# Windowed attention in front of a GELU layer: query halves of 64 with 192 keys each, instead of 128 queries with 256 keys

## The chip, the cores and the metric

The kernel runs on one core of one Trainium2 chip. The metric is the device time of one execution in microseconds (us), as the median of several runs. Five engines work side by side, each through its own instructions in order: TensorE (PE; its weight loads are listed apart as PEld), VectorE (DVE), ScalarE (ACT), GpSimd (POOL) and SyncE (SP), which here only issues loads. They wait for each other by semaphores. A matmul multiplies weights held in the array with columns that stream through it; its result goes to PSUM, which has eight banks.

## The reference

```python
# q, k, v: [4, 8, 768, 64]; n_global = 8, n_local = 96
scores = scale * np.matmul(q, k.transpose(0, 1, 3, 2))
rel = pos[:, None] - pos[None, :]
is_global = pos[None, :] < int(n_global)
is_local = (rel >= 0) & (rel < int(n_local))
keep = is_global | is_local
dist = np.where(is_global & ~is_local, float(n_local), np.abs(rel))
scores = scores + (-slopes[:, None, None] * dist[None])       # slopes: one per head
scores = np.where(keep, scores, -1000000000.0)
a = softmax(scores)                                           # over the keys
attn_out = np.matmul(a, v)
x = attn_out.transpose(0, 2, 1, 3).reshape(4 * 768, 512)
h = x @ w_in                                                  # 512 -> 2048
g = 0.5 * h * (1.0 + erf(h * inv_sqrt2))
return (g @ w_out).astype(np.float32)                         # 2048 -> 512
```

A query sees at most the 96 keys that end at its own place, and the first 8 keys of its sequence.

## The kernel before

The 3072 rows are cut into 12 chunks of 256 rows (`c`); three chunks make one sequence of the batch, so chunks 0, 3, 6 and 9 are a sequence's first ("first chunks") and the others are "later chunks". A chunk has four pairs of heads (`p`); the two heads of a pair (`hh`) lie in partitions 0 to 63 and 64 to 127 of the transposed queries and keys. Within a chunk `j` is the half of 128 queries.

Per pair, attention goes through these steps. `load` (L241) issues the loads of q, k and v on SP, six for a pair of a later chunk and three for one of a first chunk. `split` (L274) scales the queries on POOL. `scores_pair` (L281) multiplies: for each `j` and head, 128 queries by 256 keys (in a later chunk 32 keys from the start of the sequence and the 224 keys from 96 before the half to its end; in a first chunk the first half has 128 keys and the second 256). The product is fp32, with 64 rows and 128 weight columns, so the two heads of a pair use the upper and the lower half of the array's rows. VectorE adds the mask `pen` and finds the row minimum (L305). `exps` (L315) takes the exponentials on ScalarE, sums them, and scales by the inverse sums on POOL (on VectorE for chunks 0 and 1). `flip` (L339) transposes the probabilities in blocks of 128 by 128 on PE, four a head (three in a first chunk), and ScalarE copies them out of PSUM. `av_pair` (L353) multiplies the values, 128 keys by 64 columns as weights, with these blocks, so that the two heads use the left and the right half of the array's columns. ScalarE evicts the sum (`xh`, L382) and VectorE takes the rest (`xl`, L158).

The GELU layer runs in steps `T`, each of one slice `s` of 256 of the 2048 inner columns and one chunk: `m1` (L385, `h`, 24 matmuls), `gelu` (L400, twice on ScalarE) and `m2` (L411, `acc`, 12 matmuls of 512 columns). Chunks 0 and 1 take turns by slice while the weights come in; from chunk 2 on a chunk's eight slices follow each other. The weights arrive as 64-bit words in 32 pieces of 512 KB (`load_weights`, four a slice), which ScalarE and VectorE take apart (L188 to L212).

Which step of attention stands beside which GELU step is set by tables of offsets:

```python
EVS = {"load": (-4, -3, 0, 1), "split": (-2, -1, 2, 3), "s": (0, 0, 4, 4), "pt": (2, 3, 6, 7), "av": (4, 4, 8, 8)}
EVENTS = [EVF, EVF, EV2] + [EVS] * (NCH - 3)
```

From chunk 3 on (`EVS`), every fourth step has a block: av of two pairs, then s of two pairs, in one run on PE. Chunk 2 (`EV2`) goes pair by pair, and chunks 0 and 1 (`EVF`) stand ahead of the GELU steps. Tiles in PSUM come from a pool of six banks (`ps`), taken in turn; `acc` has two of its own. In `run` SP's order begins with chunk 0, the four pieces of weight slice 0, the four pairs of chunk 1, and then the slices 1 to 6. A scheduler sets the final order on each engine.

## Time and profile before

| what | value |
|---|---|
| runs | 719.08, 717.80, 718.84 us; median 718.84 |
| profiled execution, first to last instruction (span) | 719.0 us |
| PE busy | 695.4 us (97%), 4909 matmul records |
| PEld busy | 612.0 us (85%) |
| ACT busy | 371.4 us (52%) |
| DVE busy | 291.4 us (41%) |
| POOL busy | 114.9 us (16%) |
| DMA | 68.03 MB, mean 95 GB/s |
| TensorE's granted clock | 0.987 of full speed as a mean |

The span is that of one profiled execution, and the runs beside it lie within 1.3 us of it, so sums made from the profile can be set against the runs directly. Busy time of PE counts overlapping matmuls once, and a matmul's end is modelled; how fast PE really goes is read from the starts of the blocks, not from busy time.

### The profile page before, as it was taken

The numbers are of one execution on the slowest core, as the hardware profiler recorded it, in microseconds if no ns is written. First come the engines' busy times: TensorE is split into PE (matmuls) and PEld (weight loads), VectorE is DVE, ScalarE is ACT, GpSimd is POOL, SyncE is SP. The second block draws the span as 40 slices with busy tenths as digits, with TensorE's granted clock in tenths as the row PEclk, the third lists the DMA queues.
The fourth block names the chain that finished last, engine by engine and source line by source line (L and its number), as shares of the span: only waits on it lengthen the run. The fifth ranks groups of instructions, "written<-read, shape, count | busy, mean of one in ns | idle before, by whom it ended". The sixth has DMA issues, their size and how long they took to land.

```text
span 719.0 us, 12918 instructions
## 1 busy us (share of the span) xinstructions
PE 695.4 (97%) x4909; PEld 612.0 (85%) x4909; DVE 291.4 (41%) x957; ACT 371.4 (52%) x838; POOL 114.9 (16%) x227
## 2 busy tenths in 40 slices
PE   7888989999999999999999999999999999999996
PEld 4567878788898898899898898988988988998895
DVE  6988988612423324323323324133243243231110
ACT  4885678826535626536436446356356365453211
POOL 3001123302202202012022022022022020120000
PEclk9998999999999999999999999999999999999999
DMA  8527863304324313204224223223233221000000
GB/s 284 156 88 233 264 185 139 111 8 132 103 66 126 104 58 119 74 30 130 80 71 134 90 72 101 84 67 89 88 103 103 88 74 31 30 2 1 31 0 34
DMA packets 60901, 68.03 MB, mean 95 GB/s; under 512 B 13472, under 2 KB 49312, under 8 KB 60832
## 3 DMA queue, kind: packets, MB, share of 16 engines
q1 hardware_dynamic: 56560, 59.92, 28.3%
q10 hardware_dynamic: 4272, 7.21, 2.7%
q8 instruction: 41, 0.67, 0.4%
q14 instruction: 28, 0.23, 0.1%
HBM read 60.82 MB, written 6.29 MB: 93 GB/s over the span
## 4 chain that ended last, share of the span: by engine, by line
PE 84%; ACT 6%; DVE 3%; DMA 3%; POOL 1%; issue 1%; ACTq 0%; DVEq 0%; SPq 0%; POOLq 0%
PE h L396 35%; PE acc L426 34%; PE av L370 5%; PE s L295 5%; PE t L346 5%; ACT n L322 3%; DMA w<-w 2%; POOL n L331 1%; ACT L322 1%; ACT w L188 1%; DVE wb L198 1%; DVE wb L196 1%; DVE n L331 1%; DMA nn_w<-limits 0%; DVE wb L194 0%
## 5 line engine op out<-in xcount | busy, mean ns | idle before, releaser
L396 PE MATMUL h<-xh,winh 128*128 128x256 f32 x768 | 221.9, 289 | 0.8 <-ACT xh L382 0.8
L396 PE MATMUL h<-xl,winh 128*128 128x256 f32 x768 | 218.3, 284 | 0.0
L396 PE MATMUL h<-xh,winl 128*128 128x256 f32 x768 | 217.5, 283 | 0.0
L158 DVE TENSOR_TENSOR gl<-gr,gh 128x512 fp32r<-128x512 f32 x96 | 67.9, 707 | 344.0 <-ACT gr L407 344.0
L426 PE MATMUL acc<-wouth,gh 128*128 128x512 f32 x384 | 156.2, 407 | 4.8 <-ACT gh L406 4.8
L396 PEld LDWEIGHTS h<-xh,winh 128*128 128x128 f32 x768 | 147.6, 192 | 6.6 <-issue 1.8
L396 PEld LDWEIGHTS h<-xl,winh 128*128 128x128 f32 x768 | 147.7, 192 | 4.2 <-DVE n L331 0.3
L426 PE MATMUL acc<-woutl,gh 128*128 128x512 f32 x384 | 151.2, 394 | 0.0
L426 PE MATMUL acc<-wouth,gl 128*128 128x512 f32 x384 | 149.8, 394 | 0.1
L396 PEld LDWEIGHTS h<-xh,winl 128*128 128x128 f32 x768 | 147.4, 192 | 0.1
L406 ACT ACTIVATE gh<-h 128x512 fp32r<-128x512 f32 x96 | 57.3, 597 | 164.7 <-PE h L396 164.6
L350 ACT COPY pt<-t 128x512 f32<-128x512 f32 (+1 forms) x96 | 52.8, 553 | 110.3 <-PE t L346 110.2
L152 POOL TENSOR_SCALAR qr<-qr,qsc 128x256 f32<-128x256 f32 x48 | 28.1, 586 | 459.5 <-DMA qr<-qT 390.1
L331 POOL TENSOR_SCALAR n<-n,su 128x256 f32<-128x256 f32 (+1 forms) x160 | 83.9, 543 | 65.6 <-DVE su L325 26.7
L426 PEld LDWEIGHTS acc<-wouth,gh 128*128 128x128 f32 x384 | 72.3, 188 | 23.7 <-issue 5.8
L426 PEld LDWEIGHTS acc<-wouth,gl 128*128 128x128 f32 x384 | 72.1, 188 | 16.9 <-DVE gl L158 0.8
L426 PEld LDWEIGHTS acc<-woutl,gh 128*128 128x128 f32 x384 | 72.4, 189 | 12.8 <-issue 0.3
L322 ACT ACTIVATE n<-n,mn 128x256 f32<-128x256 f32 (+1 forms) x144 | 68.7, 479 | 0.7 <-DVE mn L305 0.5
L305 DVE CUSTOM_DVE_ANT_0 n<-s,pen 128x256 f32<-128x256 f32 (+1 forms) x192 | 65.8, 397 | 7.7 <-PE s L295 6.0
L346 PE MATMUL t<-ident,n 128*128 128x128 f32 x352 | 57.6, 282 | 5.2 <-DVE n L331 4.3
L407 ACT ACTIVATE gr<-h 128x512 f32<-128x512 f32 x96 | 56.8, 592 | 0.0
L370 PE MATMUL av<-pt,vr 128*64 128x128 f32 x704 | 51.9, 283 | 4.6 <-ACT pt L350 4.5
(68 smaller groups left out, 561.2 us busy)
## 6 DMA issues: line engine op xcount, KB each, us to landing
w<-w SPq DMA_DIRECT2D x32, 512.0 KB, 4.7
c<-w SPq DMA_DIRECT2D x32, 512.0 KB, 3.7
kr<-kT SPq DMA_DIRECT2D x32, 224.0 KB, 3.1
out<-o ACTq DMA_DIRECT2D x24, 256.0 KB, 2.0
qr<-qT SPq DMA_DIRECT2D x45, 128.0 KB, 2.8
vr<-v SPq DMA_DIRECT2D x44, 128.0 KB, 2.3
vr<-v SPq DMA_DIRECT2D x32, 96.0 KB, 2.3
kr<-kT SPq DMA_DIRECT2D x13, 128.0 KB, 2.6
```

Source lines behind the costliest of these rows:

```text
L158: return self.nc.vector.tensor_tensor(out=out, in0=in_, in1=hi.bitcast(F32), op=ALU.subtract)
L295: ins = nc.tensor.matmul(sp[hh][:, j, :w], lhsT=qq[hr, j * P:(j + 1) * P], rhs=kt[hr, 0 if first else j, :w], start=True, stop=True).ins
L305: ins = nc.vector.tensor_tensor_reduce(out=nn[:, j, :w], in0=sp[hh][:, j, :w], in1=pen, scale=-slope(2 * p + hh), scalar=3e38, op0=ALU.add ...
L322: self.table(nc.scalar.activation(out=nn[:, j, :w], in_=nn[:, j, :w], func=AF.Exp, bias=mn[:, i:i + 1], scale=-1.0, accum_out=su[:, i:i + 1]))
L331: ins = eng.tensor_scalar(out=nn[:, j, :w], in0=nn[:, j, :w], scalar1=su[:, i:i + 1], scalar2=0.0, op0=ALU.mult, op1=ALU.add)
L346: nc.tensor.transpose(tp[:, i, :], nn[:, j, a * P:(a + 1) * P], self.ident)
L350: nc.scalar.copy(pt, tp[:, :n, :])
L370: ins = nc.tensor.matmul(av[64 * hh:64 * hh + 64, j, :], lhsT=vt[hh][:, vi, :], rhs=pt[hh][:, i, :], start=(j, a) == js[0], stop=(j, a) == ...
L396: nc.tensor.matmul(hp[:, f, :], lhsT=w[:, d, f * P:(f + 1) * P], rhs=x[:, d, :], start=n == 0, stop=n == 3 * NP - 1)
L406: self.table(nc.scalar.activation(out=gh, in_=hp, func=AF.Gelu))
L407: self.table(nc.scalar.activation(out=gr, in_=hp, func=AF.Gelu))
L426: nc.tensor.matmul(acc, lhsT=g[:, f, ks], rhs=w[:, f, :], start=s == 0 and n == 0, stop=s == NST - 1 and n == 5)
```

## The change

The 128 queries of a half become two quarters of 64 (`a`). A quarter's keys are 64 + 32 + 96 = 192 (`NK`): 32 from the start of the sequence, the 96 that both quarters share around their border, and 64 of its own. The loads put the keys of a half side by side so that each quarter's 192 can be read as two runs of 96 (`pairs`). A score matmul then has 64 weight columns and 192 streamed columns, and the four matmuls of a half (two heads, two quarters) name four different quarters of the array. In a first chunk the first half of 128 queries keeps its form.

The probabilities of a half are then 192 wide, and the two halves of a head take three transposes of 128 by 128: the shared 128 keys of each half, and one block with the 64 own keys of both halves. The values are loaded in four blocks to match (two shared, two of own keys). `av_pair` multiplies the shared keys as before, and then the own keys with 64 rows, 64 weight columns and 64 streamed columns, on quarters of the array; the halves `j` go to PSUM banks of their own in later chunks, and are evicted apart. From chunk 3 on it does both pairs of a block at the second of them. A pair of a later chunk has twelve loads instead of six; the mask is one tile of 448 columns.

```diff
+def pairs(t, off, step, n):
+    return bass.AP(tensor=t.tensor, offset=t.offset + off, ap=[list(t.ap[0]), [step, 2], [1, n]])
...
+    def load_v(self, dma, vv, v0, cc, w):
+        row = lambda r, n: dap(self.v, v0 + r * DM, [[DM, n], [1, w]])
+        q0 = cc * CT
+        if cc:
+            dma(vv[0:NC, 0, :], row(q0 - 32, NC))
+            dma(vv[NC:P, 0, :], row(0, NG))
+        else:
+            dma(vv[:, 0, :], row(0, P))
+        dma(vv[0:NG, 1, :], row(0, NG))
+        dma(vv[NG:P, 1, :], row(q0 + 96, NC))
+        for j in range(2) if cc else (1,):
+            o = HQ * j if cc else 0
+            dma(vv[o:o + HQ, 2:4, :],
+                dap(self.v, v0 + (q0 + j * P - 96) * DM, [[DM, HQ], [160 * DM, 2], [1, w]]))
...
-            sync(kr[:, :, NG:256], dap(self.kT, k0 + cc * CT - 96, [[S, P], [P, 2], [1, 224]]))
-            sync(kr[:, :, 0:NG], dap(self.kT, k0, [[S, P], [0, 2], [1, NG]]))
...
+            sync(pairs(kr, NG, 352, NX + NC), dap(self.kT, q0 - 96, [[S, P], [192, 2], [1, NX + NC]]))
+            sync(kr[:, 224:288], dap(self.kT, q0 + HQ, [[S, P], [1, NX]]))
+            sync(kr[:, KW:KW + NX], dap(self.kT, q0 + 32, [[S, P], [1, NX]]))
+            for o in (0, 192):
+                sync(pairs(kr, o, 352, NG), dap(self.kT, k0, [[S, P], [0, 2], [1, NG]]))
+        self.load_v(sync, vr.rearrange("p n h d -> p n (h d)"), v0, cc, P)
...
         for j in range(2):
-            w = P if first and j == 0 else 256
-            for hh in range(2):
-                hr = slice(hh * D, hh * D + D)
-                ins = nc.tensor.matmul(sp[hh][:, j, :w], lhsT=qq[hr, j * P:(j + 1) * P],
-                                       rhs=kt[hr, 0 if first else j, :w], start=True, stop=True).ins
...
+            for a in range(1 if first and j == 0 else 2):
+                for hh in range(2):
+                    hr = slice(hh * D, hh * D + D)
+                    if first and j == 0:
+                        out, lhs, rhs = sp[hh][:, 0, 0:P], qq[hr, 0:P], kt[hr, 0:P]
+                    else:
+                        o = j * P + a * HQ
+                        out, lhs = sp[hh][a * HQ:(a + 1) * HQ, j, :], qq[hr, o:o + HQ]
...
-        tp = self.bank([P, 4, P], f"t{c}_{h}")
-        for i, (j, a) in enumerate(pts):
-            nc.tensor.transpose(tp[:, i, :], nn[:, j, a * P:(a + 1) * P], self.ident)
+        tp = self.bank([P, 3, P], f"t{c}_{h}")
+        for i, o in enumerate((0, 2 * P, NK if c % CPB == 0 else P)):
+            nc.tensor.transpose(tp[:, i, :], nn[:, o:o + P], self.ident)
...
+        if first:
+            avb = self.bank([P, 2, n, P], f"av{c}_{p}")
+            av = [avb[:, j] for j in range(2)]
+        else:
+            av = [self.bank([P, n, P], f"av{c}_{p}_{j}") for j in range(2)]
...
+        for i in range(n):
+            for j in range(2):
+                for hh in range(2):
+                    pt, vt = heads[i, hh]
+                    add(av[j][hh * D:(hh + 1) * D, i, :], vt[:, j, :], pt[:, j, :],
+                        i == 0 and (j == 0 or not first), first and j == 0)
+        for i in range(n):
+            for a in range(2):
+                for j in range(2):
+                    if first and j == 0:
+                        continue
+                    ks = slice(0, HQ) if first else slice(j * HQ, (j + 1) * HQ)
+                    for hh in range(2):
+                        pt, vt = heads[i, hh]
+                        qs = slice(a * HQ, (a + 1) * HQ)
+                        add(av[j][hh * D:(hh + 1) * D, i, qs], vt[ks, 2 + a, :], pt[ks, 2, qs], False, True)
+        for j in range(2):
+            xh, xl = (x[:, ps.start:ps.stop, j * P:(j + 1) * P] for x in self.x[c])
+            nc.scalar.copy(xh, av[j])
+            self.lo_dve(xl, av[j], xh)
```

Lines shift: what is L295 (s), L346 (t), L370 (av), L396 (h) and L426 (acc) before stands at L337, L382, L412, L449 and L479 in the changed kernel.

On PE, this is the block in chunk 4 in which av of the pairs 0 and 1 and s of the pairs 2 and 3 follow each other, as it stood before. A name such as `s4_6` is the tile of chunk 4, head 6; the size is that of the output.

```order
L370 MATMUL av4_0_2698<-pt4_0_2552,vr4_0_2062 64x128 x8
L370 MATMUL av4_0_2698<-pt4_2_2611,vr4_1_2181 64x128 x8
L295 MATMUL s4_4_2719<-kr4_2_2353,qr4_2_2354 128x256
L295 MATMUL s4_5_2720<-kr4_2_2353,qr4_2_2354 128x256
L295 MATMUL s4_4_2719<-kr4_2_2353,qr4_2_2354 128x256
L295 MATMUL s4_5_2720<-kr4_2_2353,qr4_2_2354 128x256
L295 MATMUL s4_6_2733<-kr4_3_2470,qr4_3_2471 128x256
L295 MATMUL s4_7_2734<-kr4_3_2470,qr4_3_2471 128x256
L295 MATMUL s4_6_2733<-kr4_3_2470,qr4_3_2471 128x256
L295 MATMUL s4_7_2734<-kr4_3_2470,qr4_3_2471 128x256
L426 MATMUL acc3_0_2578<-wouth2_712,gh29_2625 128x512
```

The same block on PE in the changed kernel, up to the first scores of pair 2:

```order
L412 MATMUL av4_1_0_2925<-pt4_0_2776,vr4_0_2239 64x128 x2
L412 MATMUL av4_1_1_2926<-pt4_0_2776,vr4_0_2239 64x128 x2
L412 MATMUL av4_1_0_2925<-pt4_2_2833,vr4_1_2374 64x128 x2
L412 MATMUL av4_1_1_2926<-pt4_2_2833,vr4_1_2374 64x128 x2
L412 MATMUL av4_1_0_2925<-pt4_0_2776,vr4_0_2239 64x64 x2
L412 MATMUL av4_1_1_2926<-pt4_0_2776,vr4_0_2239 64x64 x2
L412 MATMUL av4_1_0_2925<-pt4_0_2776,vr4_0_2239 64x64 x2
L412 MATMUL av4_1_1_2926<-pt4_0_2776,vr4_0_2239 64x64 x2
...
L337 MATMUL s4_4_2957<-kr4_2_2552,qr4_2_2553 64x192
L337 MATMUL s4_5_2958<-kr4_2_2552,qr4_2_2553 64x192
L337 MATMUL s4_4_2957<-kr4_2_2552,qr4_2_2553 64x192
L337 MATMUL s4_5_2958<-kr4_2_2552,qr4_2_2553 64x192
```

The 16 matmuls of av of 128 columns became 8 of 128 columns and 16 of 64; the 8 of s became 16 of half the height and 192 columns. The order of the parts is the same.

On PE, in a first chunk (chunk 3), the scores of pair 2 in the changed kernel stand between av and the scores of pair 3:

```order
L412 MATMUL av3_1_2285<-pt3_2_2193,vr3_1_1774 64x64 x4
L337 MATMUL s3_4_2308<-kr3_2_1943,qr3_2_1944 128x128
L337 MATMUL s3_5_2309<-kr3_2_1943,qr3_2_1944 128x128
L337 MATMUL s3_4_2308<-kr3_2_1943,qr3_2_1944 64x192
L337 MATMUL s3_5_2309<-kr3_2_1943,qr3_2_1944 64x192
L337 MATMUL s3_4_2308<-kr3_2_1943,qr3_2_1944 64x192
L337 MATMUL s3_5_2309<-kr3_2_1943,qr3_2_1944 64x192
L337 MATMUL s3_6_2324<-kr3_3_2057,qr3_3_2058 128x128
```

Here matmuls of the old form (128 rows of output) and of the new one follow each other in turn.

On SP, the loads of the last pair of chunk 1 and the first pieces of weight slice 1 stood like this before:

```order
L246 DMA qr_3_199<-qT 128x256
L246 DMA kr_3_198<-kT 128x2x224
L246 DMA kr_3_198<-kT 128x2x32
L246 DMA vr_3_200<-v 128x2x128
L246 DMA vr_3_200<-v 96x2x128
L246 DMA vr_3_200<-v 32x2x128
L163 DMA w_0_207<-w 128x1024
L163 DMA w_1_209<-w 128x1024
```

and stand like this in the changed kernel:

```order
L279 DMA qr_3_226<-qT 128x256
L279 DMA kr_3_225<-kT 128x2x160
L279 DMA kr_3_225<-kT 128x64 x2
L279 DMA kr_3_225<-kT 128x2x32 x2
L279 DMA vr_3_227<-v 96x128
L279 DMA vr_3_227<-v 32x128 x2
L279 DMA vr_3_227<-v 96x128
L279 DMA vr_3_227<-v 64x2x128 x2
L178 DMA w_0_240<-w 128x1024
L178 DMA w_1_242<-w 128x1024
```

Twelve loads stand where six stood, for each of the four pairs, and the weights of slice 1 come behind all of them as before.

## Rows read from the trace of the kernel before

**Rows 1.** The head of the page, and its chain of work that ended last: shares of the span by engine and by line.
```profile
span 719.0 us, 12918 instructions
...
PE 84%; ACT 6%; DVE 3%; DMA 3%; POOL 1%; issue 1%; ACTq 0%; DVEq 0%; SPq 0%; POOLq 0%
PE h L396 35%; PE acc L426 34%; PE av L370 5%; PE s L295 5%; PE t L346 5%; ACT n L322 3%; DMA w<-w 2%; POOL n L331 1%; ACT L322 1%; ACT w L188 1%; DVE wb L198 1%; DVE wb L196 1%; DVE n L331 1%; DMA nn_w<-limits 0%; DVE wb L194 0%
```

**Rows 2.** Busy time by stretch of the span: start and end, length, then PE, PEld, DVE, ACT and POOL busy with the number of instructions, the granted clock of TensorE, the DMA engines' share and GB/s.
```profile
0.00:30.00 30.00, 22.66 (x124) 14.74 (x125) 22.12 (x93) 17.13 (x56) 7.96 (x27) 0.89 0.79 246
30.00:60.00 30.00, 25.63 (x194) 19.79 (x194) 26.94 (x83) 24.05 (x58) 0.00 (x0) 0.94 0.35 107
60.00:95.00 35.00, 30.22 (x180) 26.55 (x179) 29.51 (x59) 24.20 (x44) 8.13 (x7) 0.95 0.81 247
95.00:130.00 35.00, 34.11 (x224) 28.49 (x224) 28.86 (x64) 27.01 (x55) 11.86 (x13) 0.95 0.48 154
130.00:700.00 570.00, 569.94 (x4123) 511.51 (x4122) 182.60 (x661) 275.62 (x623) 87.00 (x181) 1.00 0.26 75
```

**Rows 3.** Who PE waited for over the whole span, longest first: us in total, times, longest us.
```profile
PE acc L426 <- ACT gh L406: 4.8, 2, 2.4
PE av L370 <- ACT pt L350: 4.5, 4, 2.0
PE t L346 <- DVE n L331: 4.3, 3, 2.3
```

**Rows 4.** The chain in order of time around a block of a later chunk: start us, us, what, and how many records.
```profile
291.53 0.44 PE t L346 x4
291.96 2.75 PE acc L426 x12
...
297.58 1.90 PE av L370 x32
299.48 1.93 PE s L295 x16
301.41 2.95 PE acc L426 x12
```

**Rows 5.** The same around a block of a first chunk.
```profile
347.30 0.33 PE t L346 x3
...
353.27 1.46 PE av L370 x24
354.73 1.51 PE s L295 x16
```

**Rows 6.** Groups of ScalarE's instructions with different shapes kept apart, over the whole span: line, operation, output<-input, shapes, count | busy us, mean ns of one | idle us before and what ended it.
```profile
L406 ACT ACTIVATE gh<-h 128x512 fp32r<-128x512 f32 x96 | 57.3, 597 | 164.7 <-PE h L396 164.6
L407 ACT ACTIVATE gr<-h 128x512 f32<-128x512 f32 x96 | 56.8, 592 | 0.0
...
L382 ACT CAST xh<-av 128x256 fp32r<-128x256 f32 x12 | 4.3, 360 | 12.2 <-PE av L370 12.1
```

**Rows 7.** SP's issues in order of time while chunk 1 is loaded: start us, us, and how many of one line and tile follow each other. The rows between are the pairs' loads of k and v.
```profile
5.12 0.43 SPq L246 DMA_DIRECT2D qr<-qT  x1
...
12.43 0.35 SPq L246 DMA_DIRECT2D qr<-qT  x1
...
16.20 0.42 SPq L246 DMA_DIRECT2D qr<-qT  x1
...
19.18 0.42 SPq L246 DMA_DIRECT2D qr<-qT  x1
...
22.21 1.30 SPq L163 DMA_DIRECT2D w<-w  x2
```

**Rows 8.** From the rows of the weight pieces `w` between 20 and 45 us: the time from issue to landing.
```profile
DMA to landing us min/median/max: 3.5/3.6/4.7
```

**Rows 9.** ScalarE takes the first piece of weight slice 1: its row in order of time on ScalarE (a wait would stand in brackets), and its row in the chain.
```profile
33.19 0.66 ACT L188 ACTIVATE w<-w 128x512 int32<-128x512 uint32 x1
...
33.28 0.56 ACT w L188
```

**Rows 10.** Groups of ScalarE's and VectorE's instructions between 0 and 60 us with shapes kept apart, columns as in rows 6.
```profile
L322 ACT ACTIVATE n<-n,nmax 128x256 f32<-128x256 f32 x24 | 11.9, 498 | 0.7 <-DVE nmax L305 0.6
L350 ACT COPY pt<-t 128x512 f32<-128x512 f32 x8 | 4.4, 575 | 2.0 <-PE t L346 2.0
L350 ACT COPY pt<-t 128x384 f32<-128x384 f32 x8 | 3.6, 467 | 0.8 <-PE t L346 0.8
L322 ACT ACTIVATE n<-n,nmax 128x128 f32<-128x128 f32 x8 | 3.1, 394 | 9.2 <-DVE nmax L305 9.2
...
L305 DVE CUSTOM_DVE_ANT_0 n<-s,pen 128x256 f32<-128x256 f32 x24 | 9.3, 418 | 0.6 <-POOL pen L135 0.6
L331 DVE TENSOR_SCALAR n<-n,su 128x256 f32<-128x256 f32 x24 | 7.3, 348 | 0.1
L331 DVE TENSOR_SCALAR n<-n,su 128x128 f32<-128x128 f32 x8 | 2.4, 302 | 0.1
L305 DVE CUSTOM_DVE_ANT_0 n<-s,pen 128x128 f32<-128x128 f32 x8 | 2.3, 284 | 0.4 <-PE s L295 0.4
```

**Rows 11.** The chain in order of time between 100 and 130 us, one step on POOL: start us, us, what.
```profile
109.15 3.55 POOL n L331 x3
```

**Rows 12.** Busy time in the middle of an av block of a later chunk, columns as in rows 2.
```profile
326.00:327.40 1.40, 1.40 (x30) 1.40 (x28) 0.44 (x1) 0.93 (x2) 0.00 (x0) 1.00 0.00 0
```

More of the change, by code (lines that the diff above doesn't have):

```diff
@@ L23 @@
 NG = 32
+HQ = 64
+NX = 64
+NC = 96
+NK = NX + NG + NC
+KW = NC + 2 * (NX + NG)
 CT = 256
@@ L288, in scores_pair @@
         kt, qq = self.kt.pop((c, p)), self.qt.pop((c, p))
[L289 removed]
+        sp = [self.bank([P, 2, NK], f"s{c}_{2 * p + hh}") for hh in range(2)]
         prev = self.last_av if EVENTS[c] is not EVF else None
         for j in range(2):
[L292 to L299 removed]
+            for a in range(1 if first and j == 0 else 2):
[7 more added lines that the diff above has]
+                        if first:
+                            rhs = pairs(kt[hr, :], 192 if a else 288, -96 if a else -192, NC)
+                        elif j == 0:
+                            rhs = pairs(kt[hr, :], 96, 96 if a else -96, NC)
+                        else:
+                            rhs = pairs(kt[hr, :], KW + 192 * a, -96 if a else 96, NC)
+                    ins = nc.tensor.matmul(out, lhsT=lhs, rhs=rhs, start=True, stop=True).ins
+                    if prev is not None:
+                        self.after(ins, prev, "heads and halves in turn")
+                    prev = ins
@@ L318, in exps @@
         mn, su = self.stat.pop((c, p))
-        every = [(self.pt_n[c, 2 * p + hh], j, P if first and j == 0 else 256, 2 * hh + j)
+        every = [(self.pt_n[c, 2 * p + hh][:, j * NK:j * NK + (P if first and j == 0 else NK)], 2 * hh + j)
                  for hh in range(2) for j in range(2)]
-        for nn, j, w, i in every:
-            self.table(nc.scalar.activation(out=nn[:, j, :w], in_=nn[:, j, :w], func=AF.Exp, bias=mn[:, i:i + 1],
+        for nn, i in every:
+            self.table(nc.scalar.activation(out=nn, in_=nn, func=AF.Exp, bias=mn[:, i:i + 1],
                                             scale=-1.0, accum_out=su[:, i:i + 1]))
@@ L359, in av_pair @@
                          self.xp.tile([P, NP, CT], F32R, name=f"xl{c}", tag="xl"))
-        pts = self.parts(c)
-        pt = [self.pt_t.pop((c, 2 * p + hh)) for hh in range(2)]
-        vt = [self.vt.pop((c, 2 * p + hh)) for hh in range(2)]
-        if p % 2 == 0 or EVENTS[c] is not EVS:
-            self.avb = self.bank([P, 2, 2, P], f"av{c}_{p}")
-        av = self.avb[:, p % 2]
-        for i, (j, a) in enumerate(pts):
-            vi = (a if first else 2 * j + a)
-            js = [x for x in pts if x[0] == j]
-            for hh in range(2):
-                ins = nc.tensor.matmul(av[64 * hh:64 * hh + 64, j, :], lhsT=vt[hh][:, vi, :], rhs=pt[hh][:, i, :],
-                                       start=(j, a) == js[0], stop=(j, a) == js[-1]).ins
-                if self.last_av is not None and i + hh > 0:
-                    self.after(ins, self.last_av, "two heads in turn")
-                self.last_av = ins
-        ps = slice(p, p + 1)
         if EVENTS[c] is EVS:
@@ L378, in av_pair, with add @@
                 return
-            ps = slice(p - 1, p + 1)
-        xh, xl = (x[:, ps, :].rearrange("d p (j q) -> d p j q", j=2) for x in self.x[c])
-        av = self.avb[:, ps.start % 2:ps.start % 2 + ps.stop - ps.start]
-        nc.scalar.copy(xh, av)
-        self.lo_dve(xl, av, xh)
+            ps = range(p - 1, p + 1)
+        else:
+            ps = range(p, p + 1)
+        n = len(ps)
+        if first:
+            avb = self.bank([P, 2, n, P], f"av{c}_{p}")
+            av = [avb[:, j] for j in range(2)]
+        else:
+            av = [self.bank([P, n, P], f"av{c}_{p}_{j}") for j in range(2)]
+        heads = {(i, hh): (self.pt_t.pop((c, 2 * q + hh)), self.vt.pop((c, 2 * q + hh)))
+                 for i, q in enumerate(ps) for hh in range(2)}
+        def add(out, lhs, rhs, start, stop):
+            ins = nc.tensor.matmul(out, lhsT=lhs, rhs=rhs, start=start, stop=stop, skip_group_check=True).ins
+            if self.last_av is not None:
+                self.after(ins, self.last_av, "heads and halves in turn")
+            self.last_av = ins
+        for i in range(n):
[18 more added lines that the diff above has]
+            self.lo_dve(xl, av[j], xh)
     def m1(self, t, f):
```

87 lines of the change are left out of this document (41 added, 46 removed).

## The prediction

> **What bounds the kernel now.** I read the page's chain first: 84% of it is TensorE, and of the lines that the change touches the chain holds av, s and t with 5% each [rows 1]. The table by stretch says where that is so: from 130 us to 700 us PE is busy for 569.94 of 570 us at granted clock 1.00, while ScalarE and VectorE are half busy or less; before 130 us PE is idle for some 17 us, with VectorE and DMA the fuller ones at different times [rows 2]. So there are two regimes. Behind 130 us a microsecond off PE's attention blocks is a microsecond off the end; ahead of it, it is worth that only where PE is what the others wait for. PE is idle there for softmax results, for copies and for Gelu inputs [rows 3].
>
> In the first regime the chain gives the price of every block directly, without modelled ends. A block of two pairs in a chunk that is not a batch's first ("later chunk") costs av 1.90 us and s 1.93 us, and each head's four transposes cost 0.44 us; the products with w_out just behind s take 2.95 us instead of 2.75 us [rows 4]. In a batch's first chunk the same block is av 1.46, s 1.51, and three transposes 0.33 us [rows 5].
>
> **Unit prices, from differences of these blocks.** The trace has two matmul records for each such fp32 matmul of the program: 32 for 16 in av. Two heads run side by side, so two records make one slot.
> - av: (1.90 - 1.46) / 8 records = 55 ns a record, 110 ns a slot of 128 columns; 1.90 - 32 x 0.055 leaves 0.14 us for entering the block.
> - s: first and later chunks differ by 4 slots of 128 columns more: 0.42 / 4 = 105 ns for 128 columns, 0.82 ns a column. First chunk: 4 slots of 128 and 4 of 256 columns make 1.26 us, so entry costs 0.25.
> - A transpose is 0.11 us.
> So each change of the array's division costs 0.14 us into matmuls with 64 weight columns and 0.25 us into those with 128; these are taken for the new changes too.
>
> **The change on PE.** By columns, a group on four quarters should take, if all four run at once, 64 x 0.82 + 5 = 58 ns (own keys with V) or 192 x 0.82 + 4 = 160 ns (scores). No row of before shows four at once: av shows two column halves, s two row halves, each at the full rate for two.
>
> Later chunk, block of two pairs: four heads lose one transpose each, -0.44. av becomes 8 slots of 110 and 0.14 entry (1.02), then 8 groups of 58 and a change of division, 0.14 (0.60): 1.62 against 1.90, -0.28. s has 8 groups of 160 instead of 8 slots; it follows on the same quarters, so it pays no entry: 1.28 against 1.93, -0.65. Sum **-1.37 us**. That is the low end. At the high end the 64-column groups go no faster than today's narrowest slot, 110 ns: +0.42, so -0.95. I take -1.25, nearer the low end, because in s the slot does shrink in proportion to its columns. The exit to w_out stays, since the array changes its division there now as well.
>
> First chunk, block of two pairs: transposes unchanged. av: 4 of its 12 slots become 8 of 64 columns (half the array: there is one row half only) and one more change: 8 x 0.110 + 0.14 + 8 x 0.058 + 0.14 = 1.62 against 1.46, +0.16. s: per pair 2 slots of 128 columns and 2 groups of 160, and because the first 128 queries keep the old form, the array changes its division four times in the block: 2 x 0.54 + 0.25 + 0.14 + 0.25 + 0.14 = 1.86 against 1.51, +0.35. Sum **+0.5 us** a block: in these chunks the change loses.
>
> Six later chunks (4, 5, 7, 8, 10, 11) have two blocks each: 12 x -1.25 = -15.0. Three first chunks (3, 6, 9): 6 x +0.5 = +3.0. Chunk 2 is done in single pairs between 80 and 140 us, where PE still waits elsewhere; I count half of two blocks, -1.2. PE: **-13.2 us**. With the low end everywhere and chunk 2 in full it is -16.1; with the high end (a first block then +0.9) and nothing for chunk 2, -5.9.
>
> **The other engines behind 130 us.** Exponentials, reductions, normalisation and copies of P become narrower, the eviction of av becomes two; they are off the chain there and hidden under PE's work, with ScalarE busy 275.62 of 570 us [rows 2]; without that cover each block's second eviction would cost its 0.36 us [rows 6]. One more PSUM bank per block is held by av, of six: the last s tile then needs the bank of h of the same step, which Gelu gives back after two reads of 0.6 us [rows 6], while that s is due over 2 us after h ends. SP issues 12 loads instead of 6 for a later pair, at about 0.5 us each 24 us in a chunk of 55.7 us (from the av block of [rows 4] to that of [rows 5] are two blocks, eight steps): hidden, since a load stands two steps ahead of the scaling of its queries.
>
> **The opening, 0 to 130 us.** Here the loads are not hidden. SP issues 24 loads for chunk 1 before the second weight slice; the third and fourth pair take 2.98 us for six, 0.50 us an issue, and the first of the weights goes at 22.21 us [rows 7]. With 48 loads, 24 x 0.50 = 12 us at most; the first two pairs took 7.3 and 3.8 us, longer than six issues, so part is covered by bytes on the way, and I put the weights at 31 to 34 us. They take 3.6 us to land [rows 8]. ScalarE takes that piece at 33.19 us, without a wait and on the chain [rows 9]: it would stall 2 to 4.6 us, and behind it stand, in order, the cast of w_out, the evictions of av and the copies of P for chunk 1, so PE's first MoE step too. Against that, ScalarE and VectorE get through earlier. Their means up to 60 us [rows 10]: an exponential 498 ns at 256 columns, 394 at 128, so 52 less at 192, 24 times, 1.2 us, and 8 copies of P at 108 less, 0.9; VectorE's reductions 67 less, 24 times, 1.6 us, and its scaling 23 less, 0.6. The split eviction takes about 1 us back on each. Later the chain passes through POOL's scaling, 3.55 us for three [rows 11]; 192 columns take about 0.9 off, twice, with one PE gap of similar size. Net I take **+1.5 us**, with -2 (relief, no stall) and +5 (full stall kept) as bounds. Chunk 2's 24 extra issues between 57 and 80 us stand among weight pieces; in the new order most pieces have as many loads ahead of them as before, the last of slice 4 has ten more.
>
> **Sum.** The profiled span is 719.0 us, the runs' median 718.84, 0.2 below it. 719.0 - 13.2 + 1.5 - 0.2 = 707.1: **707 us**; the bounds of all terms together give 701 to 718 for this case.
>
> **Rivals.**
> *Two at a time (732 us, slower).* The quarters of one row half wait for each other, or the two row halves do. Then a later block is av 1.02 + 0.14 + 16 x 0.058 = 2.09, s 16 x 0.160 = 2.56, transposes -0.44: +0.38; a first block has s 2.50 against 1.51: +1.15 with av. 12 x 0.38 + 6 x 1.15 + 0.5 + 1.5 = +13.5. It decides once a 192-column group of four takes more than some 250 ns. For it: no row shows four. Against it: the halves of either direction already run at the full rate [rows 4, 5], and four quarters read and write no more per cycle than these two forms do, one at a time. The Trainium skill (TensorE: Matmul & The Clock Gate, "Measured speedup vs the span model") has row and column packing compose, 10.6 times for 16 tiles; no run here shows it yet.
>
> *Records come no faster than now (724 us, slower).* The densest stretch has 30 records in 1.40 us, 47 ns each [rows 12]. If that is issue and not the array, 32 records of 64 columns take 1.50, and 32 of s 1.50: later block -0.11, first block +0.9; 12 x -0.11 + 6 x 0.9 + 1.5 = +5.6. Against it: 110 ns a slot is what 128 columns cost in s too, where records are half as dense.
>
> *A price per program instruction (712 us).* By the program's order these 30 records are 15 instructions, so one instruction may take up to 93 ns to issue. A group of four 64-column instructions has 2 x 58 ns of columns, 29 ns each; halfway to the bound, at 61 ns, the 16 of a block take 0.98 us instead of 0.46, while s (80 ns each) stays bound by columns: later block -0.85, and 12 x 0.4 + 0.4 makes 5 us less gain than forecast. The Trainium skill (same page, "Wait — 56ns, not 53.3ns?") states about 62 ns per MATMUL where the sequencer decodes in microcode. Counted per record, the 47 ns above speak against that; counted per instruction, no row here does.
>
> *The opening loses more (716 us).* Both sets of 24 extra issues reach the chain, 5 + 5 us, nothing given back.
>
> **How the numbers follow.** Forecast 0.60; opening 0.10; price per instruction 0.08; records 0.08; two at a time 0.14. About 0.2% (1.4 us) is what a measurement here can tell from no change. Faster: 0.60 + 0.08 + 0.08 of the opening's and 0.01 of the records' = 0.77; same 0.05, from the opening's and the records' edges; slower 0.18. Range: the case's own is 701 to 718, so 700 to 722 leaves out two at a time and half of the records' case, two in ten.
>
> **What would show it.** In the changed kernel's chain behind 130 us: t x3 at 0.33 everywhere; av of a later block near 1.62 and s near 1.28 to 1.35; s of a first block near 1.86, longer than now; s starting without a step behind av. In the opening: the first load of slice 1 at 31 to 34 us on SP and a wait of ScalarE for it. The prediction is wrong if s of a later block is above 1.9 (rivals of pace), if PE shows waits behind 130 us (banks, loads), or if PE becomes full much later than 130 us.

## Result and the profile after

The changed kernel takes 723.88 us (median of nine runs, 722.55 to 724.53) where the kernel before, run beside it, takes 718.84: the ratio is 1.007, with a 95% interval of 1.0053 to 1.0087. It is 0.7% slower. The forecast was 707 us. One run of e3 below took 3633 us; its median and ratio are those of the other three.

The head of the page and the chain of the changed kernel, for [rows 1]:

```profile
span 722.7 us, 14534 instructions
...
PE 83%; DMA 6%; ACT 3%; SPq 3%; DVE 2%; POOL 1%; issue 1%; ACTq 0%; POOLq 0%; DVEq 0%
PE h L449 35%; PE acc L479 35%; PE av L412 5%; PE s L337 5%; PE t L382 4%; DMA w<-w 3%; SPq L279 3%; DMA kr<-kT 2%; ACT n L363 1%; POOL n L372 1%; DVE wb L211 1%; DMA nn_w<-limits 1%; DVE wb L213 0%; ACT w L203 0%; ACT L363 0%
```

SPq L279, the issue of loads, is new in the chain with 3%; before, SP had 0%. The table by stretch, columns as in [rows 2]:

```profile
0.00:30.00 30.00, 21.24 (x150) 13.55 (x150) 20.64 (x90) 14.93 (x50) 9.28 (x31) 0.83 0.71 200
30.00:60.00 30.00, 17.79 (x144) 13.07 (x146) 14.65 (x58) 15.49 (x45) 0.48 (x1) 0.77 0.38 121
60.00:95.00 35.00, 29.17 (x238) 25.01 (x228) 27.63 (x64) 21.41 (x47) 2.90 (x2) 0.95 0.54 170
95.00:130.00 35.00, 29.01 (x204) 23.38 (x203) 29.49 (x67) 26.18 (x54) 11.18 (x11) 0.90 0.77 256
130.00:700.00 570.00, 568.79 (x4675) 506.01 (x4674) 190.95 (x711) 276.58 (x668) 84.68 (x187) 1.00 0.29 81
```

From 30 to 60 us PE is busy for 17.79 us instead of 25.63 and VectorE for 14.65 instead of 26.94: in that stretch the engines wait. The chain around a block of a later chunk and one of a first chunk, for [rows 4] and [rows 5]:

```profile
284.11 1.65 PE av L412 x48
285.76 1.30 PE s L337 x32
287.06 2.99 PE acc L479 x12
...
365.62 1.64 PE av L412 x32
367.25 1.82 PE s L337 x24
369.07 2.99 PE acc L479 x12
```

The rows from 365.62 us are a block of chunk 6, a first chunk. These are close to the prices that were forecast. So the gain is there, and more than that is lost in the opening. To put a number on both, the run is cut where PE starts the first product with w_in of chunk 3: at 219.45 us before, at 235.98 us after. Behind that point the kernel before takes 499.56 us to its end and the changed one 486.77. The change gains **12.8 us behind** the cut and loses **16.5 us ahead** of it. (These are the two profiled executions, 3.7 us apart; the medians are 5.0 apart, so some 1.3 us are outside this account.)

Ahead of it, three views show the way of the loss. SP's issues in order of time, for [rows 7] (start, us, count of one line and tile):

```profile
5.17 4.07 SPq L178 DMA_DIRECT2D w<-w  x4
9.28 0.43 SPq L279 DMA_DIRECT2D qr<-qT  x1
...
19.33 0.59 SPq L279 DMA_DIRECT2D qr<-qT  x1
...
26.38 0.59 SPq L279 DMA_DIRECT2D qr<-qT  x1
...
32.77 0.59 SPq L279 DMA_DIRECT2D qr<-qT  x1
33.41 2.41 SPq L279 DMA_DIRECT2D kr<-kT  x5
35.86 3.16 SPq L279 DMA_DIRECT2D vr<-v  x6
39.14 33.01 SPq L178 DMA_DIRECT2D w<-w  x8
```

The first load of weight slice 1 goes at 39.14 us instead of 22.21. ScalarE in order of time, for [rows 9]; the wait stands in brackets:

```profile
36.47 0.44 ACT L363 ACTIVATE n<-n,nmax 128x192 f32<-128x192 f32 x1
...
43.14 0.67 ACT L203 ACTIVATE w<-w 128x512 int32<-128x512 uint32 x1 [6.13 <-DMA w<-w]
43.71 0.60 ACT L223 CAST wouth<-wb 128x512 fp32r<-128x512 f32 x1
44.22 0.26 ACT L435 CAST xh<-av 128x128 fp32r<-128x128 f32 x1
44.38 0.86 ACT L386 COPY pt<-t 128x384 f32<-128x384 f32 x2
45.27 0.27 ACT L435 CAST xh<-av 128x128 fp32r<-128x128 f32 x1
...
52.98 0.60 ACT L459 ACTIVATE gh<-h 128x512 fp32r<-128x512 f32 x1 [4.17 <-PE h L449]
```

ScalarE stands still for 6.13 us, waiting for that piece. Behind it stand the last two of chunk 0's eight evictions `xh`, which the first GELU step's products with w_in need, and the first copies of P for chunk 1. VectorE waits for the same piece, and behind that wait stand the last two of chunk 0's rests `xl`, which these products need too:

```profile
43.14 0.43 DVE L209 TENSOR_SCALAR wb<-w 128x512 int32<-128x512 int32 x1 [4.68 <-DMA w<-w]
...
45.75 0.28 DVE L173 TENSOR_TENSOR xl<-av,xh 128x128 fp32r<-128x128 f32 x1
```

PE's waits over the whole span, for [rows 3], and two stretches of PE behind the stall (columns as in [rows 2]):

```profile
PE av L412 <- ACT pt L386: 15.2, 7, 8.6
PE acc L479 <- ACT gh L459: 7.9, 2, 4.9
```

```profile
36.30:44.90 8.60, 0.00 (x0) 0.00 (x0) 2.78 (x9) 2.47 (x9) 0.00 (x0) 0.70 0.66 223
44.90:53.00 8.10, 8.09 (x57) 6.19 (x58) 3.42 (x15) 2.34 (x6) 0.00 (x0) 0.50 0.35 126
```

PE does nothing for 8.60 us and then works at a granted clock of 0.50, its lower level of 1.2 GHz. The first Gelu starts at 52.98 us, where it started at 38.02 before.

### The profile page after: what moved, and what is told of

Its sections match the earlier page's. It is cut to its first block, busy times and chain, and to the rows that moved or that the text cites. A ratio compares the mean times of both kernels' runs of the same rounds, so it can differ in the third digit from the quotient of the medians.

```text
span 722.7 us, 14534 instructions
## 1 busy us (share of the span) xinstructions
PE 682.6 (94%) x5485; PEld 595.3 (82%) x5485; DVE 285.4 (39%) x987; ACT 358.9 (50%) x868; POOL 108.5 (15%) x232
## 4 chain that ended last, share of the span: by engine, by line
PE 83%; DMA 6%; ACT 3%; SPq 3%; DVE 2%; POOL 1%; issue 1%; ACTq 0%; POOLq 0%; DVEq 0%
PE h L449 35%; PE acc L479 35%; PE av L412 5%; PE s L337 5%; PE t L382 4%; DMA w<-w 3%; SPq L279 3%; DMA kr<-kT 2%; ACT n L363 1%; POOL n L372 1%; DVE wb L211 1%; DMA nn_w<-limits 1%; DVE wb L213 0%; ACT w L203 0%; ACT L363 0%
## 5 line engine op out<-in xcount | busy, mean ns | idle before, releaser
L449 PE MATMUL h<-xh,winh 128*128 128x256 f32 x768 | 221.0, 288 | 0.0
L449 PE MATMUL h<-xl,winh 128*128 128x256 f32 x768 | 217.6, 283 | 0.0
L449 PE MATMUL h<-xh,winl 128*128 128x256 f32 x768 | 217.2, 283 | 0.0
L479 PE MATMUL acc<-wouth,gh 128*128 128x512 f32 x384 | 157.9, 411 | 8.0 <-ACT gh L459 7.9
L479 PE MATMUL acc<-woutl,gh 128*128 128x512 f32 x384 | 151.2, 394 | 0.0
L449 PEld LDWEIGHTS h<-xh,winh 128*128 128x128 f32 x768 | 146.8, 191 | 5.2 <-issue 1.1
L449 PEld LDWEIGHTS h<-xl,winh 128*128 128x128 f32 x768 | 147.1, 192 | 4.2 <-issue 0.5
L479 PE MATMUL acc<-wouth,gl 128*128 128x512 f32 x384 | 149.8, 395 | 0.2 <-DVE gl L173 0.2
L449 PEld LDWEIGHTS h<-xh,winl 128*128 128x128 f32 x768 | 147.0, 191 | 0.1
L372 POOL TENSOR_SCALAR n<-n,su 128x192 f32<-128x192 f32 (+1 forms) x160 | 73.3, 479 | 351.5 <-ACT n L363 206.8
L386 ACT COPY pt<-t 128x384 f32<-128x384 f32 x96 | 45.8, 481 | 101.8 <-PE t L382 101.8
L479 PEld LDWEIGHTS acc<-wouth,gh 128*128 128x128 f32 x384 | 72.7, 189 | 27.1 <-ACT gh L459 8.5
L479 PEld LDWEIGHTS acc<-wouth,gl 128*128 128x128 f32 x384 | 72.5, 189 | 17.9 <-DVE gl L173 1.1
L479 PEld LDWEIGHTS acc<-woutl,gh 128*128 128x128 f32 x384 | 72.9, 190 | 12.5
L412 PE MATMUL av<-pt,vr 64*64 64x64 f32 (+1 forms) x1024 | 49.5, 251 | 15.5 <-ACT pt L386 15.2
L363 ACT ACTIVATE n<-n,mn 128x192 f32<-128x192 f32 (+1 forms) x144 | 62.3, 434 | 1.5 <-DVE mn L346 1.3
L412 PEld LDWEIGHTS av<-pt,vr 64*64 64x64 f32 (+1 forms) x1024 | 37.3, 137 | 29.5 <-ACT pt L386 18.2
L346 DVE CUSTOM_DVE_ANT_0 n<-s,pen 128x192 f32<-128x192 f32 (+1 forms) x192 | 55.2, 341 | 11.5 <-PE s L337 11.3
L167 POOL TENSOR_SCALAR qr<-qr,qsc 128x256 f32<-128x256 f32 x48 | 30.6, 637 | 184.6 <-DMA qr<-qT 173.7
```

Source lines behind the costliest of these rows:

```text
L167: self.nc.gpsimd.tensor_scalar(out=out, in0=in_, scalar1=scale, scalar2=0.0, op0=ALU.mult, op1=ALU.add)
L346: ins = nc.vector.tensor_tensor_reduce(out=nn[:, j * NK:j * NK + n], in0=sp[hh][:, j, 0:n], in1=pen, scale=-slope(2 * p + hh), scalar=3e38 ...
L363: self.table(nc.scalar.activation(out=nn, in_=nn, func=AF.Exp, bias=mn[:, i:i + 1], scale=-1.0, accum_out=su[:, i:i + 1]))
L372: ins = eng.tensor_scalar(out=nn, in0=nn, scalar1=su[:, i:i + 1], scalar2=0.0, op0=ALU.mult, op1=ALU.add)
L386: nc.scalar.copy(pt, tp)
L412: ins = nc.tensor.matmul(out, lhsT=lhs, rhs=rhs, start=start, stop=stop, skip_group_check=True).ins
```

## The experiments

All medians of the experiments are set against runs of the kernel before on the same chip (719.1 to 719.7 us); the first two rows are from another (718.84). The table gives, from each profiled execution, SP's first load of weight slice 1, the moment ScalarE takes that piece, the first Gelu, the first product of chunk 3, and the time from there to the end; all in us.

| kernel | median | slice 1 issued | taken | first Gelu | chunk 3 | to the end |
|---|---|---|---|---|---|---|
| before | 718.84 | 22.21 | 33.19 | 38.02 | 219.45 | 499.56 |
| after | 723.88 | 39.14 | 43.14 | 52.98 | 235.98 | 486.77 |
| e1 chunks 0, 1 old | 710.77 | 22.21 | 34.03 | 38.87 | 220.55 | 487.12 |
| e2 also 3, 6, 9 old | 706.37 | 22.16 | 34.07 | 38.90 | 219.66 | 485.10 |
| e3 before, 24 issues more | 729.94 | 40.03 | 43.62 | 45.60 | 229.54 | 499.25 |
| e4 slice 1 spread ahead | 717.45 | 26.27 | 36.01 | 44.03 | 226.85 | 486.85 |
| e5 chunk 0 old | 711.45 | 36.35 | 40.29 | 43.15 | 223.57 | 486.09 |
| e6 V of chunk 1 on GpSimd | 715.64 | 25.91 | 37.10 | 46.56 | 231.25 | 486.88 |
| e7 slice 1 ahead in one | 710.39 | 26.18 | 35.96 | 42.59 | 221.76 | 486.62 |
| e8 first chunks old, V of chunk 1 on GpSimd | 703.87 | 22.03 | 33.94 | 39.40 | 217.09 | 485.91 |
| e9 evictions ahead | 716.05 | 39.19 | 43.77 | 47.74 | 228.10 | 486.54 |
| e10 and the step ahead | 720.65 | 39.90 | 43.70 | 47.77 | 233.12 | 486.48 |
| e11 e7 with first chunks old | 708.21 | 22.13 | 32.85 | 37.92 | 221.95 | 484.97 |
| e12 e8, V of chunk 2 too | 702.44 | 22.39 | 33.10 | 38.08 | 212.07 | 485.35 |

The last column has two levels: 499 for the old form and 485 to 487 for halves, where the four kernels with old first chunks (e2, e8, e11, e12) are the lowest. Everything else that differs lies ahead of chunk 3. Most edits do more than their text says: a scheduler sets the order on every engine, and only in e4 and e6 do ScalarE, VectorE and PE keep the changed kernel's order throughout.

### Where: the first two chunks (e1, e2)

Methods with `_old` are those of the kernel before; e1 has `OLD = (0, 1)`, e2 `(0, 1, 3, 6, 9)`. For want of space the second halves of chunk 1's probabilities lie in five buffers of their own.

```diff
-                        {"load": self.load, "split": self.split, "s": self.scores_pair, ...}[what](c, p)
+                        getattr(self, name + "_old" if c in OLD else name)(c, p)
```

> The changed kernel, but chunks 0 and 1 are loaded and computed in the old form (three and six loads a pair, 128 queries by 256 keys); chunk 2 and all later chunks stay in halves. Theory A (the loss lies in the opening, in the extra loads of chunks 0 and 1, which put the first load of weight slice 1 at 39.14 us instead of 22.21): that load is back at 22 to 23 us, the wait of 15.2 us for copies of P shrinks to some 5, and about all of the 17 us comes back: 706 to 709. Rival B (the loss comes from chunk 2's loads among the later weight pieces, or the narrow matmuls cost more than their blocks show): the time stays at 718 us or above. In between, 710 to 716: both have a share.

> As the run before, and the first chunks of the other sequences (3, 6, 9) in the old form too. Their block cost 1.65 + 1.82 us in halves against 1.46 + 1.51 before, 0.50 more, in six blocks. Theory A: 3 us less than the run before, 703 to 706, with av at 1.46 and s at 1.51 in these chunks again. Rival (blocks side by side with other work, so that a block's price in the chain does not add up to time): less than 1 us from the run before.

e1 takes 710.77 us (ratio 0.9882, 0.9856 to 0.9908), above theory A's 706 to 709 and at the lower edge of the case in which both have a share; its opening is within 1.1 us of before. So nearly all of the loss comes from chunks 0 and 1 (13.1 us by the medians, 15.4 by the cut), and chunk 2 has at most a small share. e2 takes 706.37, just above its 703 to 706 and 4.4 us less than e1. The two traces are 2.9 us apart, about the 3 that was expected: 0.9 ahead of the cut, where chunk 3's blocks stand, and 2.0 behind it, 0.5 for each of the four blocks of the chunks 6 and 9. The chain in e2 at a block of chunk 6:

```profile
348.94 1.46 PE av L563 x24
350.40 1.51 PE s L493 x16
```

The old prices of [rows 5] are back: halves cost time in a first chunk, as forecast. (As a mean over all traces of the table it is 0.3 us a block: 486.7 to the end with halves there, 485.3 with the old form.)

### What: issues on SP ahead of slice 1 (e3 to e7)

e3 is the kernel before, where the program changes only the number of issues (the scheduler then gives ScalarE, VectorE and PE other orders too):

```diff
+            if c == 1:
+                n = out.ap[0][1] // 2
+                nc.sync.dma_start(out[0:n], in_[0:n])
+                return nc.sync.dma_start(out[n:2 * n], in_[n:2 * n])
```

> The kernel before, where each of the 24 loads of chunk 1 is issued as two loads of half the partitions: the same bytes in the same runs, the same matmuls, 24 issues more on SP ahead of weight slice 1. Theory A (what counts is SP's time for an issue, 0.4 to 0.6 us each): the first load of slice 1 goes at 32 to 36 us instead of 22.21 and the kernel takes 727 to 732 us. Rival B (issues are hidden under bytes on the way, and it is the changed sizes or the late start of chunk 0 that count): 718 to 721 us.

It takes 729.94 us, 10.8 more than before (ratio 1.0128, 1.0096 to 1.016), inside theory A's range; slice 1 goes 4 us later than A said. Its rows on SP:

```profile
24.48 1.64 SPq L248 DMA_DIRECT2D qr<-qT  x1
26.16 0.60 SPq L249 DMA_DIRECT2D qr<-qT  x1
26.81 0.62 SPq L248 DMA_DIRECT2D kr<-kT  x1
```

The same bytes in twice as many loads put slice 1 at 40.03 us and make the kernel before slower than the changed one. Nothing of the new arithmetic is needed for a loss of this size.

e4 and e7 change only SP's order in the changed kernel: slice 1's four pieces come behind the second pair of chunk 1, spread among the later loads by the scheduler in e4, and in one piece in e7.

```diff
             self.load(1, p)
+            if p == 1:
+                for i in range(4):
+                    self.load_weights(1, i)
...
+            if c == 1 and p > 1:
+                self.after(ins.ins, self.word_ins[1, 3], "behind slice 1")
```

(The last two lines are e7's alone.)

> The changed kernel, where SP issues the first piece of weight slice 1 behind two pairs of chunk 1 instead of four, and the other three pieces among the loads of the third and fourth pair. Nothing else moves. Theory A1 (the late first pieces of slice 1 hold up ScalarE's order): the first piece goes at about 23 us, and 5 us or more come back: 712 to 719. Rival A2 (chunk 1's own queries, keys and values being late is what holds up the softmax of chunk 1 and with it everything behind): 722 to 725, since those only get later by the issues of four pieces.

> The changed kernel, where all four pieces of weight slice 1 go on SP ahead of the third and the fourth pair of chunk 1. The run with the pieces spread among these pairs had the first at 26.27 us and the fourth at 40.76 and gave 6.4 us back. Theory A1 (ScalarE's order waits for the pieces): the fourth goes at about 28 us and 3 us more come back, 712 to 715. Rival A2 (now the third and fourth pair's own data are what is late: they come some 4 to 6 us later): 718 to 724.

e4 takes 717.45 us (ratio 0.9977, 0.9954 to 1.0), inside A1: one changed order on one queue, with every load, byte and product kept and the order on all other engines too, brings 6.4 us back. e7 takes 710.39 (ratio 0.9903, 0.9873 to 0.9933), better than A1 asked for, 13.5 us below the changed kernel, although the fourth piece goes at 35.86 us and not at 28. Here the scheduler moved work on ScalarE, VectorE and PE as well (first on PE, just ahead of the first Gelu), so these 13.5 us are not the order on SP alone: the first Gelu comes only 1.4 us sooner than in e4, chunk 3 comes 5.1 sooner. A2 falls for e7: SP issues the third and fourth pair's own data some 10 us later in e7, at 36.24 and 43.29 us, and the kernel gains all the same. ScalarE takes the piece without a wait:

```profile
35.96 0.64 ACT L203 ACTIVATE w<-w 128x512 int32<-128x512 uint32 x1
...
42.59 0.60 ACT L461 ACTIVATE gh<-h 128x512 fp32r<-128x512 f32 x1 [1.19 <-PE h L451]
```

e5 has `OLD = (0,)`; e6 leaves the loads on SP but for the V of chunk 1:

```diff
...
+        prev = self.hi_pool(qr, qr, self.qsc[:, p:p + 1])
+        if c == 1:
+            def pool(out, in_):
+                self.after(self.nc.gpsimd.dma_start(out, in_).ins, prev, "behind the scaling")
+            self.load_v(pool, vr.rearrange("p n h d -> p n (h d)"), self.v0[p], 1, P)
```

> The changed kernel with chunk 0 alone in the old form (three SP loads ahead of the weights instead of five, 256 keys for 128 queries); chunk 1 has its twelve loads a pair. In the changed kernel SP began with chunk 1 at 9.28 us instead of 5.12, so that start is a quarter of the 16.9 us by which the weights of slice 1 came late. Theory A (every us on SP ahead of slice 1 counts): slice 1 goes at 34 to 36 us, the first product of chunk 3 starts 3 to 5 us sooner than the 235.98 us of the changed kernel, and the time is 718 to 721. Rival (only chunk 1's issues count, chunk 0's loads only use a wait for bytes): 722.5 to 724.5.

> The changed kernel, where the six loads of V of each pair of chunk 1 are issued by GpSimd, behind the scaling of the pair's queries, instead of by SP; all bytes, sizes and matmuls stay. Theory A (SP's issue time ahead of slice 1): six issues a pair on SP, so slice 1 goes at about 26 us, and 10 us or more come back if GpSimd's issues are not slower than SP's: 710 to 715. Rival B (the small transfers themselves, not who issues them): 722 to 725. Rival C (GpSimd takes over 1 us an issue, so that the scaling of the next pair's queries, which stands behind them, is late): 715 to 722.

e6 takes 715.64 us, 8.2 below the changed kernel and just above A's 710 to 715; its runs reach from 712.5 to 719.9, and its profiled one is the slowest. C's range has that time but its condition did not come: six issues take GpSimd 3.27 to 3.45 us, under 0.6 each. So who issues counts, and B (the small transfers themselves) falls. e5 missed: 711.45 us (ratio 0.9905, 0.9885 to 0.9925) where 718 to 721 was expected. Slice 1 goes only 2.8 us sooner than in the changed kernel and ScalarE still waits 6.11 us for it, yet 12.4 us come back. The theory that the loss is SP's lateness, microsecond for microsecond, falls with that. The rows of e5 show what is different:

```profile
33.44 0.36 ACT L575 CAST xh<-av 128x256 fp32r<-128x256 f32 x1
33.69 0.48 ACT L387 COPY pt<-t 128x384 f32<-128x384 f32 x1
40.29 0.67 ACT L207 ACTIVATE w<-w 128x512 int32<-128x512 uint32 x1 [6.11 <-DMA w<-w]
...
43.15 0.60 ACT L602 ACTIVATE gh<-h 128x512 fp32r<-128x512 f32 x1
```

Chunk 0's last eviction, of four here, stands ahead of the stall. PE is through with all 24 products of the first step at 36.5 us, and Gelu comes 2.9 us behind the piece instead of 9.8.

### Why so dear: what stands behind the stall (e9, e10)

That makes a new theory, D: the stall is 6 us, but it costs 15 because of what ScalarE's order has behind it. e9 keeps every load and moves the piece behind these evictions (the first copies of P then stand ahead of it too):

```diff
+        if (s, i) == (1, 0):
+            self.after(ins, self.last_xh, "behind the evictions of chunk 0")
```

and e10 adds to each av of chunk 1's first pair:

```diff
+            if (c, p) == (1, 0):
+                self.after(ins, self.last_h, "behind the first step")
```

> The changed kernel with one edge more: on ScalarE, the first piece of weight slice 1 is taken behind the last evictions of chunk 0 instead of ahead of them (the scheduler then puts the first copies of P of chunk 1 ahead of it too). All loads, their order on SP and all sizes stay, so that piece still goes at about 39 us and ScalarE still waits some 6 us for it. Theory D (the wait itself was 6.1 us, but it stood in front of the evictions that the first step's h needs, and so put the first Gelu at 52.98 us, 15 us later than before): the first Gelu comes at 44 to 47 us, the first product of chunk 3 at 226 to 230 instead of 235.98, the time is 713 to 718. Rival E (the pieces of slices 1 and 2 are late for their own steps, whatever stands behind the wait): 721 to 725.

> As the run before, and on TensorE the first av of chunk 1 stands behind the last h of the first step (in the changed kernel 16 of the step's 24 products with w_in stood behind that av). Theory D: the first Gelu comes at 44 to 46 us, right behind the wait, and not behind chunk 1's evictions; the time is within 2 us of the run before, 712 to 717, since both orders have the step through at the end of the wait. Rival E: 721 to 725. If chunk 1's softmax is the longer chain, this run is slower than the one before by 2 us or more.

```profile
39.09 0.27 ACT L437 CAST xh<-av 128x128 fp32r<-128x128 f32 x1 [0.88 <-DVE xl L173]
43.77 0.67 ACT L203 ACTIVATE w<-w 128x512 int32<-128x512 uint32 x1 [4.41 <-DMA w<-w]
...
47.74 0.60 ACT L461 ACTIVATE gh<-h 128x512 fp32r<-128x512 f32 x1 [1.68 <-PE h L451]
```

e9 takes 716.05 us (ratio 0.9959, 0.994 to 0.9978): slice 1 goes at 39.19 us as in the changed kernel, and 7.8 us come back, as D said; E falls. The first Gelu comes 5.2 us sooner, at 47.74 us and not D's 44 to 47, since VectorE's wait for the piece is still there (4.72 us) with the last `xl` behind it:

```profile
44.45 0.58 PE L451 MATMUL h<-xl,winh 128*128 128x256 f32 x1 [2.45 <-DVE xl L173]
```

e10 has the same first Gelu, but takes 720.65, 4.6 more than e9, where D asked for 712 to 717. So D holds for the first Gelu and not for the whole time. e10's expectation named this case (2 us or more) with chunk 1's softmax as the longer chain. That is not shown: e10 holds back chunk 1's av, but e9 differs from it also in the order of later work on ScalarE, VectorE and PE, which the scheduler changed in e9 and hardly in e10.

### A kernel that beats both (e8, e11, e12)

e8 has `OLD = (0, 3, 6, 9)` and e6's loads of V; e11 the same `OLD` and e7's order, all loads on SP; e12 is e8 with `c in (1, 2)` where e6's edit has `c == 1`.

> First chunks (0, 3, 6, 9) in the old form, all later chunks (1, 2, 4, 5, ...) in halves, and chunk 1's loads of V issued by GpSimd as in the run before the last. It differs from the run at 706.4 us in chunk 1 alone, which is in halves here. Theory A: SP has six issues a pair ahead of slice 1, as before, so slice 1 goes at 22 to 23 us; the narrower softmax of chunk 1 gives ScalarE and VectorE back some 1 to 2 us in the opening: 704 to 707. If GpSimd's issues cost over 1 us each: 708 to 714.

> First chunks (0, 3, 6, 9) in the old form, later ones in halves, all loads on SP, and the four pieces of weight slice 1 ahead of the third pair of chunk 1. It joins the two edits that each brought the opening back (chunk 0 in the old form, 711.5 us; slice 1 ahead, 710.4 us) and takes the old form in chunks 3, 6 and 9 (2 to 4 us). If the two share one cause (the first pieces of slice 1 behind 48 issues of SP), their gains do not add: 705 to 708. If they are separate losses, they add and the kernel goes below 700.

> The kernel at 703.87 us (first chunks old, V of chunk 1 issued by GpSimd), with V of chunk 2 issued by GpSimd as well, so that SP has no more issues among the weight slices 3 to 6 than before. If chunk 2's 24 extra issues cost the opening 1 to 2 us: 701 to 703. If they are hidden: 703 to 705. If GpSimd's issues stand in the way of its scaling of chunk 2's probabilities, which is in the chain of the kernel before with 3.55 us for three: 706 or more.

e8 takes 703.87 us (ratio 0.9793, 0.9771 to 0.9814), just under theory A's 704 to 707. Six of GpSimd's issues take 3.27 to 3.64 us here, six of SP's for V in the changed kernel 3.16 to 3.91:

```profile
14.51 3.51 POOL L314 DMA_DIRECT2D vr<-v  x6
```

e11 takes 708.21 us, at the upper edge of its first case: what e5 and e7 gained does not add. That by itself does not show one cause, because what A2 feared has come in e11, where the third pair's loads go at 36.06 us:

```profile
40.83 0.90 PE L340 MATMUL s<-kr,qr 64*64 64x192 f32 x4 [3.35 <-DMA kr<-kT]
```

e12 is the fastest with 702.44 us (ratio 0.9758, 0.973 to 0.9786), inside its first case. Its interval overlaps with e8's, so what chunk 2's issues cost in the opening is not told apart from nothing; its profiled execution, with a span of 697.4 us, is the fastest of its runs (699.6 to 704.9), so its row of the table shows it at its best.

## Why the prediction was wrong, step by step

**The price of the blocks: right.** A later block went from 1.90 + 1.93 to 1.65 + 1.30 us (1.38 at another one), with 1.62 + 1.28 as the forecast's low end; a first chunk's block takes 1.64 + 1.82 (forecast 1.62 + 1.86), and e1 and e2 give 0.5 us for it (0.3 as the mean over all traces; forecast +0.5). With the four transposes saved, a later block gains 1.32 us (1.24 at the other one), where 1.25 was taken and 1.37 was the low end: groups on four quarters run near the low end. Behind the cut stand twelve later blocks, less one s of chunk 4, and four first ones: -12.4 by the forecast's prices; -12.8 was measured.

**The rivals of pace: refuted.** Two at a time would have put s at 2.56 us and equal records at 1.50; it is 1.30 to 1.38. A price per instruction would have put av at 2.14 (16 instructions in 0.98 us instead of 0.46); it is 1.65. Both together take 2.95 to 3.03 us, where the three rivals come to 4.65, 4.16 and 3.42. The rule of the Trainium skill (TensorE: Matmul & The Clock Gate, "Measured speedup vs the span model") that row and column packing compose is now shown by rows of this kernel: the s of a later block took 1.93 us on two row halves and takes 1.30 to 1.38 on four quarters.

**The other engines behind 130 us: right.** PE is busy for 568.79 of 570 us, and of the 1.2 us that lack nearly all lie ahead of 150 us (18.83 of 20 us busy there).

**The opening, +1.5 us with bounds of -2 and +5: wrong; this is the step that failed.** With chunk 2's share, chunk 3's two blocks and that s of chunk 4 the forecast had some 0.7 us ahead of the cut, and 16.5 came. Its links, in the forecast's order:
- *"so part is covered by bytes on the way, and I put the weights at 31 to 34 us."* Nothing was covered. SP's stretch for chunk 1 grew from 17.1 us (5.12 to 22.21) to 29.9 (9.28 to 39.14), 12.8 us for 24 issues, a little more than the 12 that was called the most.
- Chunk 0 was left out. SP has five loads instead of three ahead of weight slice 0, and began with chunk 1 at 9.28 instead of 5.12 us: 4.2 more.
- *"it would stall 2 to 4.6 us"*. ScalarE was itself 3.7 us later at that point (36.82 against 33.10 us at the start of the last of these reads of an exponential's sum), and it still waited for 6.13. VectorE's wait for the same piece, 4.68 us, is no term of the forecast.
- *"behind it stand, in order, the cast of w_out, the evictions of av and the copies of P for chunk 1, so PE's first MoE step too."* (That step is the first GELU step.) This names the mechanism and then prices it at the stall's own length. From the piece to the first Gelu took 9.8 us instead of 4.8, because the evictions that the step needs stood behind the stall, because PE's order has chunk 1's av and 10 records of s ahead of the step's last 15 products, and because PE came back at 1.2 GHz. 3.7 + 6.1 + 5.0 = 14.8 of the 15.0 us by which the first Gelu is late. In e9, with the evictions ahead of the piece, the first Gelu comes 4.0 us behind it. How much of the 16.5 us each of these links is worth by itself is not taken apart: e4 and e6, which have slice 1 sooner on SP and keep the orders elsewhere, bring 6.4 and 8.2 us back.
- The relief from narrower softmax is not shown: e8, with chunk 1 in halves and slice 1 on time, reaches chunk 3 2.6 us before e2, but the intervals of their medians (703.87 and 706.37) overlap.

**The rival "the opening loses more"** had the right place and 5 + 5 us; 16 came, since its bound was again the stall and not what the stall holds. Half of its price lay in chunk 2, which by e1 has at most a small share. Of the signs that the prediction names, the wait of ScalarE came; slice 1 went behind its 31 to 34 us, and PE is full a little later than 130 us.

## What to carry to other kernels

A change that pays on the bound engine can be undone by the number of loads that it takes: count issues per queue up to the first transfer that the start of the pipeline waits for, with no discount for bytes on the way unless a row shows it, and look for those of earlier tiles too. A stall is not worth its own length: read, on the engine that stalls, what stands behind the waiting instruction, follow it to the first product that needs it, and price that. And a transfer that everything waits for should stand ahead of bulk loads that nobody needs yet; here that order alone was worth 6.4 us (e4), and 13.5 together with the other orders that the scheduler then chose (e7). An edit of one queue's order is therefore read together with the order that every other engine got.
